# Two attention-fed MLPs on one core: seven early units by way of DRAM for eight, another priority for their loads of x, and one planning dependency of a hidden step

## The chip, the cores and the metric

The kernel runs on one core of a Trainium2 chip. Its time is the device time of one execution in microseconds (us); lower is better. Before the change the median of three runs is 1110.57 us (1105.44 to 1111.51). The engines are TensorE (PE), VectorE (DVE), ScalarE (ACT), GpSimd (POOL) and SyncE (SP, which here only issues DMA).

## The reference: what is computed

A causal attention with a memory term gives x (2304 rows of 512). x goes through a gated MLP of 12 units of 128 hidden columns, and its result through a second MLP of 16 such units.

```python
def reference(**kwargs):                       # cut
    # q, k, v: 4 batches x 8 heads x 576 x 64
    a = softmax(causal(scale * q @ k.T))
    attn_out = g * (phi(q) @ M_prev / (phi(q) @ z_prev)) + (1 - g) * (a @ v)
    x = attn_out.transpose(0, 2, 1, 3).reshape(2304, 512)

    gate = x @ w_gate                          # 512 -> 1536
    x = (gate * sigmoid(gate) * (x @ w_val)) @ w_out

    h = x @ w_in                               # 512 -> 2048
    g = where(h >= 1, h, where(h <= -1, 0, (h + 1) ** 2 / 4))
    return g @ moe2_w_out
```

## The kernel before

**Numbers.** Each fp32 product is made of three float32r matmuls of high and low parts (`PARTS`). The weights come as 64-bit words: a raw tile of 512 KB is loaded (L939), then decoded in some nine small steps, most of them on DVE (L946 to L964, L977, L984; ACT has L944 and L981), into a unit `wu` with a high and a low part.

**Two plans.** The program is written by a list scheduler, `Plan`: operations are added with an engine, an assumed duration, a priority (lower goes first), dependencies and buffer uses. The plan simulates the engines and emits one fixed order per engine; on the chip each engine's queue is in order, and waits are on the data and buffers alone. A dependency given to the plan only for its own sake thus moves an operation in the order and adds no wait on the chip. The first plan holds the attention; of MLP1 it holds the gate and value products of units 0 to 5 for the first three of five token groups (`groups`: 0-512, 512-1024, 1024-1536, 1536-1920, 1920-2304). The second plan holds all that follows, from about 347 us on.

**Early units.** For MLP1's units 0 to `D1`-1, the gate and value products are made early, group by group (`early_unit`): PE multiplies (L1036), ACT copies the result to a tile `gvo` (L1082), and SP stores it to the DRAM tensor `gv[f]` (L1095). In the second plan, the two late groups (1536-1920 and 1920-2304) get units 0 to D1-1, and after them the three groups of 512 get units 6 to D1-1. `load_x` (L1099) loads the four tiles of x (`xb`, 512 KB each for 512 tokens) for a group and tells the plan its priority (L1180). Weight loads of this stretch have priorities from -20 up.

**MLP1** goes in five blocks of tokens (`BLOCKS1`: 512, 512, 384, 384, 512). For each unit, `hidden` makes the hidden tile `h`: a unit below D1 loads its gate and value from `gv` (L1207, `kind` 0, into a buffer of the pool `xb`), a unit from D1 on computes them (L1036, `kind` 1). Then come five steps: ACT (L1230 or L1232), DVE (L1236 or L1238), DVE (L1242 or L1244), ACT's cast (L1248), DVE's low part (L1251). `down` (L1274) multiplies h with w_out and sums in the banks `acc`. At a block's end ACT (L1304) and DVE (L1308) evict, and SP stores y (L1315). The order of units in block 1 is `FIRST`, in the others `fs_last`. The first step of a hidden tile is planned not before the last down but one (L1253).

**MLP2** goes in five blocks (`BLOCKS2`: 512, 512, 512, 384, 384) over 16 units (`kind` 2); its weights are decoded meanwhile, as buffers come free. The result is copied (L1340) and stored (L1343).

Buffers: `xb` 9 (x tiles and gv loads share them), `raw` 3, `hp` (h) 3, `tp` (t) 2, `op` (gvo, yo, oo) 4, four PSUM banks `mm` and four `acc`.

Of the kernel before, what the change touches and what calls it, by code (L numbers as in the profile page):

```python
# [25 lines left out]
NT = B * S  # L26
D0 = 6

D1 = 8
UNITS1 = 12  # L30
EXACT = 4
EXACT_Q = 4
# [49 lines left out]
def f32(ap):  # L82
    return ap.bitcast(F32)
# [160 lines left out]
def c_act(n):  # L244
    return 0.833 * n + 53
# [10 lines left out]
def e_pe(n, cols):  # L256

    return n * (max(cols, 320) + 32) / 2.4
# [6 lines left out]
def e_dve2(n):  # L265
    return 1.04 * n + 157


def e_act(n):
    return 0.833 * n + 194  # L270
# [761 lines left out]
def up_matmuls(nc, out, unit, x, cols, kts=range(KT)):  # L1032

    for kt in kts:
        for i, (pw, px) in enumerate(PARTS):
            nc.tensor.matmul(out, kt_of(unit, pw, kt), x[kt][:, px, cols], start=(kt == 0 and i == 0),  # L1036
                             stop=(kt == KT - 1 and i == 2))
# [3 lines left out]
def tile_attention_two_moe(  # L1041
# [13 lines left out]
    xs = dram.tile([P, KT, 2, NT], F32, name="xs")  # L1055
    ys = dram.tile([P, KT, 2, NT], F32, name="ys")
    gv = [dram.tile([P, 2, NT], F32, name=f"gv{f}") for f in range(D1)]
    tables = {"gate": ({}, moe_w_gate, in_cols), "val": ({}, moe_w_val, in_cols), "wout": ({}, moe_w_out, out_rows)}
# [40 lines left out]
    def load_x(plan, src, pool, tag, tok, prio, deps=()):  # L1099


        n = tok.stop - tok.start
        s = {"x": [None] * KT, "i": [], "t": []}
        last = xlast.get(plan)
        for kt in range(KT):
            i_x = plan.inst(tag)

            def f(kt=kt):
                s["x"][kt] = pool.tile([P, 2, n], F32R, name=tag, tag=tag)
                nc.sync.dma_start(f32(s["x"][kt]), src[:, kt, :, tok])  # L1110

            s["i"].append(i_x)
            s["t"].append(plan.dma(prio, [n * 2.85], f, list(deps[kt]) if deps else [], [i_x], last))
            last = xlast[plan] = plan.last
        return s


    with ExitStack() as actx:
        plan = Plan(over=50)
# [10 lines left out]
        for b in range(B):  # L1130
            t_x[b] = [at.pair(b, n) for n in range(NP)]
            for tok in [g for g in groups if (g.stop - 1) // S == b < B - 1]:
                stored = [[t_x[e][kt] for e in range(tok.start // S, b + 1)] for kt in range(KT)]
                xh = load_x(plan, xs, fpool, "xh", tok, X_AT[b], stored)
# [8 lines left out]
    plan = Plan({"PE": 19000, "ACT": 19000, "DVE": 4000, "POOL": 6000, "DMA": 10000})  # L1143
    UNITS2 = 2 * F2 - UNITS1
    pool = lambda name, bufs: ctx.enter_context(tc.tile_pool(name=name, bufs=bufs, reuse_waits="tile"))
    xb, hp, tp = pool("xb", XB), pool("hp", HP), pool("tp", TP)
# [15 lines left out]

    first = [(kind, f) for f in range(D0, D1) for kind in ("gate", "val")]
    first += [(kind, f) for f in FIRST for kind in ("gate", "val", "wout") if (kind, f) not in ready + first]
# [4 lines left out]
    for i, ((kind, f), tag) in enumerate(zip(first, tags)):  # L1169
        table, w, cut = tables[kind]  # L1170
        table[f] = wts.decode(plan, tag, cut(w, f), -20 if i < 2 * (D1 - D0) else 10 * FIRST.index(f) - 10,
                                act=i >= NOACT)
# [4 lines left out]
        left += [place[x] for x in (("gate", f), ("val", f), ("wout", f)) if x in place]  # L1177
    late = [g for g in groups if (g.stop - 1) // S == B - 1]
    for h, tok in enumerate(late + [g for g in groups if g not in late]):
        xh = load_x(plan, xs, xb, "xb", tok, h - 50 if h < 2 else 22 + h)  # L1180
        for f in [f for f in range(D1) if tok in late or f >= D0]:
            early_unit(plan, mm, f, tok, xh, op, 25 + h, "yo", "op")

# [11 lines left out]
    def hidden(f, tok, base, x, kind, ahead=0):  # L1195


        n = tok.stop - tok.start
        s = {"i": plan.inst("hp")}
        i_t = plan.inst("tp")  # L1200
        src = []
        if kind == 0:
            i_g = plan.inst("xb")

            def load():
                s["gv"] = xb.tile([P, 2, n], F32, name="gv", tag="xb")
                nc.sync.dma_start(s["gv"], gv[f][:, :, tok])  # L1207

            src = [(lambda j=j: s["gv"][:, j], i_g) for j in range(2)]
            t_g = [plan.dma(base - 25, [n * 2.85], load, uses=[i_g], behind=xlast.get(plan))] * 2  # L1210
            xlast[plan] = plan.last
        else:
            units = (gate[f], val[f]) if kind == 1 else (w_in[f],)
            banks = [plan.inst("mm") for _ in units]

            def prod():
                for j, u in enumerate(units):
                    s[j] = mm.tile([P, HT], F32, name="mm", tag=f"mm{banks[j].slot}")
                    up_matmuls(nc, s[j][:, 0:n], u, x["x"], slice(0, n))

            t_g = [plan.add("PE", e_pe(len(units) * 12, n), base + 1 - ahead, prod,
                            [u["t"] for u in units] + x["t"], banks + [u["i"] for u in units] + x["i"],
                            behind=(ups or [None])[-1])]
            ups.append(t_g[0])
            src = [(lambda j=j: s[j][:, 0:n], i_p) for j, i_p in enumerate(banks)]

        def first_step():
            s["t"] = tp.tile([P, n], F32, name="t", tag="t")
            if kind == 2:
                nc.scalar.activation(s["t"], src[0][0](), AF.Relu, bias=half, scale=0.5)  # L1230
            else:
                nc.scalar.activation(s["t"], src[0][0](), AF.Sigmoid)  # L1232

        def second():
            if kind == 2:
                nc.vector.scalar_tensor_tensor(s["t"], s["t"], 1.0, s["t"], op0=ALU.min, op1=ALU.mult)  # L1236
            else:
                nc.vector.tensor_mul(s["t"], src[0][0](), s["t"])  # L1238

        def third():  # L1240
            if kind == 2:
                nc.vector.tensor_max(s["t"], s["t"], src[0][0]())  # L1242
            else:
                nc.vector.tensor_mul(s["t"], s["t"], src[1][0]())  # L1244

        def hi():
            s["h"] = hp.tile([P, 2, n], F32R, name="h", tag="h")
            nc.scalar.copy(s["h"][:, 0], s["t"])  # L1248

        def lo():  # L1250
            nc.vector.tensor_sub(s["h"][:, 1], s["t"], f32(s["h"][:, 0]))  # L1251

        t = plan.add("ACT", e_act(n) + 60, base, first_step, [t_g[0]] + ([] if ahead else downs[-2:-1]), [src[0][1], i_t])  # L1253
        t = plan.add("DVE", e_dve2(n), base, second, [t], [src[0][1], i_t])
        t = plan.add("DVE", e_dve2(n), base, third, [t, t_g[-1]], [src[0][1], src[-1][1], i_t])
        t = plan.add("ACT", e_act(n), base, hi, [t], [i_t, s["i"]])
        s["done"] = plan.add("DVE", e_dve2(n), base, lo, [t], [i_t, s["i"]])
        return s

    ups, downs = [], []  # L1260
# [22 lines left out]
    base = 0  # L1283
    for tok in blocks(BLOCKS1):
        n = tok.stop - tok.start
# [5 lines left out]
        for at_, f in enumerate(fs):  # L1291
            s = hidden(f, tok, base + 10 * at_, x, 0 if f < D1 else 1)

# [4 lines left out]
        for m in range(KT):  # L1298
# [11 lines left out]
            t = plan.add("ACT", c_act(n), base + 110, hi, [t_d], [i_o, i_l, state["i"][m]])  # L1310
# [11 lines left out]
    base = 50000  # L1322
    for tok in blocks(BLOCKS2):
        n = tok.stop - tok.start
# [9 lines left out]
        for m in range(n // P):  # L1334
# [10 lines left out]
            t = plan.add(("ACT", "DVE")[m % 2], c_dve2(DM), base + 200, copy, [t_d], [i_o, state["i"][m]])  # L1345
# [34 lines left out]
```

## Time and profile before

| what | value |
|---|---|
| median of three runs | 1110.57 us (1105.44 to 1111.51) |
| the profiled execution | 1110.57 us |
| its span | 1108.8 us |
| mean granted TensorE clock | 0.995 |
| PE busy | 1076.6 us, 97% of the span |
| DVE, ACT, POOL busy | 756.6, 565.4, 257.0 us |
| DMA, mean over the span | 141 GB/s |

The span is the part of the execution in which the trace has instructions; 1.8 us lie around it. Busy PE is counted from modelled ends of pipelined matmuls, so a row's duration can lap over the next row's start. In the rows of the timeline, what stands in brackets is the idle time of that engine just before the instruction and what ended it. The granted clock is 1.00 at TensorE's upper level of 2.4 GHz and half of that at its lower one.

### The profile page before, as it was taken

The numbers are of one execution on the slowest core, as the hardware profiler recorded it, in microseconds if no ns is written. First come the engines' busy times: TensorE is split into PE (matmuls) and PEld (weight loads), VectorE is DVE, ScalarE is ACT, GpSimd is POOL, SyncE is SP. The second block draws the span as 40 slices with busy tenths as digits, with TensorE's granted clock in tenths as the row PEclk, the third lists the DMA queues.
The fourth block names the chain that finished last, engine by engine and source line by source line (L and its number), as shares of the span: only waits on it lengthen the run. The fifth ranks groups of instructions, "written<-read, shape, count | busy, mean of one in ns | idle before, by whom it ended". The sixth has DMA issues, their size and how long they took to land.

```text
span 1108.8 us, 16480 instructions
## 1 busy us (share of the span) xinstructions
PE 1076.6 (97%) x5520; PEld 924.7 (83%) x5520; DVE 756.6 (68%) x1699; ACT 565.4 (51%) x1286; POOL 257.0 (23%) x325
## 2 busy tenths in 40 slices
PE   6997999999999999999999999999999999999998
PEld 4565788888888998888789997888888888889997
DVE  5688989888983788798945559999433443343433
ACT  6888889999884254544433334454222222222222
POOL 6898669666653000000000000000000000000000
PEclk9999999999999999999999999999999999999999
DMA  5567545765725889976635567361300110110000
GB/s 138 156 172 187 146 123 150 209 165 127 234 91 173 289 302 320 345 235 202 212 104 176 166 221 246 111 236 57 110 1 1 57 39 1 43 39 1 29 1 29
DMA packets 148325, 156.42 MB, mean 141 GB/s; under 512 B 70160, under 2 KB 109072, under 8 KB 148240
## 3 DMA queue, kind: packets, MB, share of 16 engines
q1 hardware_dynamic: 147664, 154.31, 44.8%
q8 instruction: 44, 0.72, 0.3%
q10 hardware_dynamic: 576, 1.05, 0.2%
q14 instruction: 41, 0.34, 0.1%
HBM read 105.78 MB, written 42.47 MB: 134 GB/s over the span
## 4 chain that ended last, share of the span: by engine, by line
PE 50%; DVE 1%; DMA 0%; issue 0%; ACT 0%; DVEq 0%
PE acc L1274 27%; PE mm L1036 23%; DMA ys<-yo 0%; DVE t L1238 0%; DVE h L1251 0%; DVE wA L956 0%; DVE t L1244 0%; DVE wu L984 0%; DVE wA L977 0%; ACT yo L1304 0%; DVE yo L1308 0%; DVE wS L961 0%; DVE wA L949 0%; DVE wA L952 0%; ACT oo L1340 0%
## 5 line engine op out<-in xcount | busy, mean ns | idle before, releaser
L1036 PE MATMUL mm<-xb,wu 128*128 128x512 f32 (+1 forms) x1968 | 410.7, 363 | 0.0
L1036 PEld LDWEIGHTS mm<-xb,wu 128*128 128x128 f32 x1968 | 357.4, 188 | 42.0 <-DVE t L1242 0.2
L1274 PE MATMUL acc<-wu,h 128*128 128x512 f32 x864 | 208.1, 390 | 0.0
L1274 PEld LDWEIGHTS acc<-wu,h 128*128 128x128 f32 x864 | 161.8, 188 | 32.3
L1248 ACT CAST h<-t 128x512 fp32r<-128x512 f32 (+1 forms) x140 | 80.9, 578 | 180.6 <-DVE t L1242 90.1
L1274 PE MATMUL acc<-h,wu 128*128 128x512 f32 (+1 forms) x720 | 152.6, 368 | 2.4 <-DVE h L1251 2.4
L1236 DVE SCALAR_TENSOR_TENSOR t<-t 128x512 f32<-128x512 f32 (+1 forms) x80 | 51.0, 638 | 146.9 <-ACT t L1230 146.9
L1274 PEld LDWEIGHTS acc<-h,wu 128*128 128x128 f32 x720 | 131.0, 188 | 20.5 <-DVE h L1251 3.7
L1251 DVE TENSOR_TENSOR h<-t,h 128x512 fp32r<-128x512 f32 (+1 forms) x140 | 89.0, 636 | 71.8 <-ACT h L1248 71.5
L1230 ACT ACTIVATE t<-mm,half 128x512 f32<-128x512 f32 (+1 forms) x80 | 51.5, 644 | 147.6 <-PE mm L1036 147.2
L1036 PE MATMUL mm<-xh,wu 128*128 128x512 f32 x432 | 115.0, 405 | 1.2 <-DMA xh<-xs 0.9
L755 POOL TENSOR_SCALAR a<-a,r,OGP 128x256 f32<-128x256 f32 (+3 forms) x144 | 96.1, 680 | 28.1 <-DVE r L746 9.7
L1036 PEld LDWEIGHTS mm<-xh,wu 128*128 128x128 f32 x432 | 77.4, 190 | 16.1 <-DMA xh<-xs 1.8
L677 ACT ACTIVATE a<-a,mn 128x128 f32<-128x128 f32 (+3 forms) x128 | 71.0, 558 | 12.7 <-DVE mn L670 12.3
L981 ACT CAST wu<-wA 128x512 fp32r<-128x512 f32 x64 | 39.7, 620 | 52.9 <-DVE wA L977 52.3
L944 ACT ACTIVATE wA<-raw 128x512 f32<-128x512 f32 x64 | 43.2, 675 | 45.3 <-DVE wu L984 20.6
L1082 ACT COPY gvo<-mm 128x512 f32<-128x512 f32 (+1 forms) x80 | 42.9, 544 | 41.3 <-PE mm L1036 40.9
L670 DVE CUSTOM_DVE_ANT_0 a<-s,mask 128x256 f32<-128x256 f32 (+3 forms) x128 | 57.7, 484 | 7.2 <-PE s L664 4.8
L397 DVE TENSOR_TENSOR R<-t,R 128x384 fp32r<-128x384 f32 (+3 forms) x120 | 53.3, 484 | 4.5 <-ACT R L393 3.7
L956 DVE SCALAR_TENSOR_TENSOR wA<-raw,wA 128x512 uint32<-128x512 uint32 x68 | 54.3, 801 | 0.6
L1242 DVE TENSOR_TENSOR t<-t,mm 128x512 f32<-128x512 f32 (+1 forms) x80 | 50.6, 632 | 2.2
L664 PE MATMUL s<-KK,SX 128*128 128x512 f32 (+3 forms) x192 | 42.0, 342 | 8.3 <-DMA KK<-KK 3.5
(134 smaller groups left out, 1401.5 us busy)
## 6 DMA issues: line engine op xcount, KB each, us to landing
raw<-in_moe_w_out_dram SPq DMA_DIRECT2D x28, 512.0 KB, 4.5
xb<-xs SPq DMA_DIRECT2D x24, 512.0 KB, 6.2
gv<-gv SPq DMA_DIRECT2D x24, 512.0 KB, 4.4
gv<-gvo SPq DMA_DIRECT2D x44, 256.0 KB, 4.6
xs<-x SPq DMA_DIRECT2D x16, 576.0 KB, 3.3
raw<-in_moe_w_in_dram SPq DMA_DIRECT2D x16, 512.0 KB
KK<-KK SPq DMA_DIRECT2D x24, 288.0 KB
raw<-in_moe_w_gate_dram SPq DMA_DIRECT2D x12, 512.0 KB, 4.7
```

The lines of the kernel that those rows point to most:

```text
L397: nc.vector.tensor_sub(lo(), src(), f32(hi()))
L670: nc.vector.tensor_tensor_reduce(a, st[f"s{h}{c}"][:, 0:kl], self.mask0[:, 512 - kl:512], -0.125, 3.0e38, ALU.add, ALU.min, mn[:, o:o + 1])
L677: nc.scalar.activation(a, a, AF.Exp, bias=mn[:, o:o + 1], scale=-1.0, accum_out=sm[:, o, 0:1])
L755: nc.gpsimd.tensor_scalar(a, a, st["mn"]["r"][:, o:o + 1], self.OGP[:, n, o:o + 1], op0=ALU.mult, op1=ALU.mult)
L956: nc.vector.scalar_tensor_tensor(s["F"], words(s["raw"])[:, :, 1], 0xC0000000, s["A"], op0=ALU.bitwise_and, op1=ALU.bitwise_or)
L1036: nc.tensor.matmul(out, kt_of(unit, pw, kt), x[kt][:, px, cols], start=(kt == 0 and i == 0), stop=(kt == KT - 1 and i == 2))
L1230: nc.scalar.activation(s["t"], src[0][0](), AF.Relu, bias=half, scale=0.5)
L1236: nc.vector.scalar_tensor_tensor(s["t"], s["t"], 1.0, s["t"], op0=ALU.min, op1=ALU.mult)
L1242: nc.vector.tensor_max(s["t"], s["t"], src[0][0]())
L1248: nc.scalar.copy(s["h"][:, 0], s["t"])
L1251: nc.vector.tensor_sub(s["h"][:, 1], s["t"], f32(s["h"][:, 0]))
L1274: nc.tensor.matmul(state[m][:, 0:o], l, r, start=(f == 0 and i == 0), stop=(f == F - 1 and i == 2), skip_group_check=True)
```

## The change

Three lines are changed. `D1` is 7 instead of 8, so that unit 7's gate and value are no longer made early and stored; each MLP1 block computes them. The loads of x for the second plan's groups have the priority h - 50 for all five groups, where the last three had 22 + h. And a hidden tile's first step is planned not before the last down but two.

```diff
--- before.py
+++ after.py
@@ -26,7 +26,7 @@
 NT = B * S
 D0 = 6
 
-D1 = 8
+D1 = 7
 UNITS1 = 12
 EXACT = 4
 EXACT_Q = 4
@@ -1177,7 +1177,7 @@
         left += [place[x] for x in (("gate", f), ("val", f), ("wout", f)) if x in place]
     late = [g for g in groups if (g.stop - 1) // S == B - 1]
     for h, tok in enumerate(late + [g for g in groups if g not in late]):
-        xh = load_x(plan, xs, xb, "xb", tok, h - 50 if h < 2 else 22 + h)
+        xh = load_x(plan, xs, xb, "xb", tok, h - 50)
         for f in [f for f in range(D1) if tok in late or f >= D0]:
             early_unit(plan, mm, f, tok, xh, op, 25 + h, "yo", "op")
 
@@ -1250,7 +1250,7 @@
         def lo():
             nc.vector.tensor_sub(s["h"][:, 1], s["t"], f32(s["h"][:, 0]))
 
-        t = plan.add("ACT", e_act(n) + 60, base, first_step, [t_g[0]] + ([] if ahead else downs[-2:-1]), [src[0][1], i_t])
+        t = plan.add("ACT", e_act(n) + 60, base, first_step, [t_g[0]] + ([] if ahead else downs[-3:-2]), [src[0][1], i_t])
         t = plan.add("DVE", e_dve2(n), base, second, [t], [src[0][1], i_t])
         t = plan.add("DVE", e_dve2(n), base, third, [t, t_g[-1]], [src[0][1], src[-1][1], i_t])
         t = plan.add("ACT", e_act(n), base, hi, [t], [i_t, s["i"]])
```

How this moves the instructions is shown at five places. First PE at the start of the second plan; `xh` rows are the last products of the first plan, `xb` rows of 384 columns those of the late groups, the first `acc` row the first down of block 1. Before:

```order
L1036 MATMUL mm<-xh,wu 128x512 x54
L1036 MATMUL mm<-xb,wu 128x384 x384
L1036 MATMUL mm<-xb,wu 128x512 x168
L1274 MATMUL acc<-h,wu 128x512 x12
L1036 MATMUL mm<-xb,wu 128x512 x24
L1274 MATMUL acc<-h,wu 128x512 x24
L1036 MATMUL mm<-xb,wu 128x512 x24
```

and with the change:

```order
L1036 MATMUL mm<-xh,wu 128x512 x54
L1036 MATMUL mm<-xb,wu 128x384 x336
L1036 MATMUL mm<-xb,wu 128x512 x120
L1274 MATMUL acc<-h,wu 128x512 x36
L1036 MATMUL mm<-xb,wu 128x512 x24
L1274 MATMUL acc<-h,wu 128x512 x36
L1036 MATMUL mm<-xb,wu 128x512 x24
```

The late groups have 48 matmuls fewer. The row of 512 columns holds, before, two units for each of three groups and one product of block 1 (144 + 24); now it holds one unit for each group and two products of block 1 (72 + 48).

PE at the border of MLP1's first two blocks; the rows `x24` and `x48` of `mm` before the last `acc` row belong to the second block, `acc` rows ahead of them to the first. Before:

```order
L1274 MATMUL acc<-h,wu 128x512 x48
L1036 MATMUL mm<-xb,wu 128x512 x24
L1274 MATMUL acc<-h,wu 128x512 x12
L1036 MATMUL mm<-xb,wu 128x512 x24
L1274 MATMUL acc<-h,wu 128x512 x48
L1036 MATMUL mm<-xb,wu 128x512 x24
```

and with the change:

```order
L1274 MATMUL acc<-h,wu 128x512 x12
L1036 MATMUL mm<-xb,wu 128x512 x24
L1274 MATMUL acc<-h,wu 128x512 x12
L1036 MATMUL mm<-xb,wu 128x512 x48
L1274 MATMUL acc<-h,wu 128x512 x36
L1036 MATMUL mm<-xb,wu 128x512 x24
```

Between the last down of the first block and the first of the second stand 48 products, where 24 stood.

SP, with the numbers of tiles: loads of x (`xb`), of raw weights and stores of early products (`gv<-gvo`) in the groups of 512. Before:

```order
L939 DMA raw_5987<-in_moe_w_out_dram 128x1024
L1095 DMA gv6_75<-gvo_6007 128x512
L939 DMA raw_6024<-in_moe_w_out_dram 128x1024
L1095 DMA gv6_75<-gvo_6022 128x512
L1110 DMA xb_6045<-xs_67 128x2x512
L1110 DMA xb_6048<-xs_67 128x2x512
L1095 DMA gv7_76<-gvo_6061 128x512
L1110 DMA xb_6075<-xs_67 128x2x512
L1110 DMA xb_6078<-xs_67 128x2x512
L1095 DMA gv7_76<-gvo_6073 128x512
L939 DMA raw_6091<-in_moe_w_out_dram 128x1024
```

and with the change, up to block 1's fourth tile (`xb_5986`):

```order
L1110 DMA xb_5899<-xs_67 128x2x512
L1110 DMA xb_5902<-xs_67 128x2x512
L939 DMA raw_5911<-in_moe_w_out_dram 128x1024
L1095 DMA gv6_75<-gvo_5913 128x512
L1110 DMA xb_5930<-xs_67 128x2x512
L1110 DMA xb_5933<-xs_67 128x2x512
L1095 DMA gv6_75<-gvo_5928 128x512
L939 DMA raw_5947<-in_moe_w_out_dram 128x1024
L1110 DMA xb_5958<-xs_67 128x2x512
L1110 DMA xb_5962<-xs_67 128x2x512
L1095 DMA gv6_75<-gvo_5971 128x512
L1110 DMA xb_5986<-xs_67 128x2x512
```

Each group has two stores where it had four, and the loads of x follow each other more closely; xb_5930 and the four after it (xb_5933, xb_5958, xb_5962, xb_5986) are the last tile of the third group and block 1's four.

PE near the end of MLP2's first block, with numbers; `mm_9023` of before and `mm_9002` of now are the product of unit 13, and the `acc` rows are downs. Before, with the first of the downs that follow:

```order
L1036 MATMUL mm_9023<-xb_8316,wu_8826 128x512 x3
L1036 MATMUL mm_9023<-xb_8319,wu_8826 128x512 x3
L1036 MATMUL mm_9045<-xb_8290,wu_8995 128x512 x3
L1036 MATMUL mm_9045<-xb_8311,wu_8995 128x512 x3
L1036 MATMUL mm_9045<-xb_8316,wu_8995 128x512 x3
L1036 MATMUL mm_9045<-xb_8319,wu_8995 128x512 x3
L1274 MATMUL acc_8638<-wu_8599,h_9041 128x512 x3
```

and with the change:

```order
L1036 MATMUL mm_9002<-xb_8151,wu_8996 128x512 x3
L1036 MATMUL mm_9002<-xb_8161,wu_8996 128x512 x3
L1036 MATMUL mm_9002<-xb_8264,wu_8996 128x512 x3
L1036 MATMUL mm_9002<-xb_8272,wu_8996 128x512 x3
L1274 MATMUL acc_8531<-wu_9021,h_9035 128x512 x3
L1274 MATMUL acc_8535<-wu_9021,h_9035 128x512 x3
L1274 MATMUL acc_8539<-wu_9021,h_9035 128x512 x3
L1274 MATMUL acc_8543<-wu_9021,h_9035 128x512 x3
L1036 MATMUL mm_9061<-xb_8151,wu_9055 128x512 x3
```

Before, the product of the next unit and the downs of earlier ones follow on the product of unit 13. Now `h_9035` is unit 13's own hidden tile, made from `mm_9002`; after it comes the product of unit 14 (`mm_9061`), and behind that `h_9093`, unit 14's own, in the same way.

DVE at that place: `t_9118` to `h_9141` are unit 13's hidden tile before, `t_9025` to `h_9035` now; the rest are steps of weights. Before:

```order
L964 SCALAR_TENSOR_TENSOR wS_9098<-raw_8978,wS_9098 128x512
L1236 SCALAR_TENSOR_TENSOR t_9118<-t_9118 128x512
L1251 TENSOR_TENSOR h_9121<-t_9096,h_9121 128x512
L1242 TENSOR_TENSOR t_9118<-t_9118,mm_9023 128x512
L977 TENSOR_TENSOR wA_9058<-wA_9058,wS_9098 128x512
L1251 TENSOR_TENSOR h_9141<-t_9118,h_9141 128x512
```

and with the change:

```order
L956 SCALAR_TENSOR_TENSOR wA_9015<-raw_8913,wA_9015 128x512
L1236 SCALAR_TENSOR_TENSOR t_9025<-t_9025 128x512
L961 TENSOR_SCALAR wS_9031<-wA_9015 128x512
L1242 TENSOR_TENSOR t_9025<-t_9025,mm_9002 128x512
L964 SCALAR_TENSOR_TENSOR wS_9031<-raw_8913,wS_9031 128x512
L949 TENSOR_SCALAR wA_9028<-wA_9028 128x512
L1251 TENSOR_TENSOR h_9035<-t_9025,h_9035 128x512
```

The chain's three steps stood with one step of a neighbour's chain and one of a decode between them; now three steps of decodes stand between them.

## Rows read from the trace of the kernel before

**Rows 1.** first part of the page: busy us (share) xinstructions

```profile
PE 1076.6 (97%) x5520; PEld 924.7 (83%) x5520; DVE 756.6 (68%) x1699; ACT 565.4 (51%) x1286; POOL 257.0 (23%) x325
```

**Rows 2.** windows of core 0: stretch, its length, then by column

```profile
core 0: us, PE busy (x) PEld busy (x) DVE busy (x) ACT busy (x) POOL busy (x), PEclk, DMA share, GB/s
...
0.00:347.00 347.00, 321.57 (x1911) 264.79 (x1912) 285.65 (x850) 300.19 (x820) 255.55 (x324) 0.99 0.57 156
...
347.00:1104.00 757.00, 754.58 (x3610) 659.88 (x3610) 470.47 (x850) 264.62 (x465) 1.44 (x1) 1.00 0.40 134
...
425.00:450.00 25.00, 25.00 (x115) 20.95 (x113) 19.76 (x38) 11.92 (x21) 0.00 (x0) 1.00 1.03 376
...
440.00:464.00 24.00, 24.00 (x107) 19.89 (x106) 17.83 (x34) 11.98 (x20) 0.00 (x0) 1.00 1.02 384
```

**Rows 3.** waits, 347 to 1109 us: who, us in total, times, longest

```profile
PE acc L1274 <- DVE h L1251: 2.4, 2, 1.4
```

**Rows 4.** timeline of PE: start, us, instruction, [idle before]

```profile
360.02 104.87 PE L1036 MATMUL mm<-xb,wu 128*128 128x384 f32 x552
...
464.73 2.88 PE L1274 MATMUL acc<-h,wu 128*128 128x512 f32 x12
...
536.95 5.74 PE L1274 MATMUL acc<-h,wu 128*128 128x512 f32 x24 [0.98 <-DVE h L1251]
```

**Rows 5.** chain that ended last, in order of time: start, us, what

```profile
590.84 4.16 PE mm L1036 x24
...
761.23 5.44 PE mm L1036 x24
```

**Rows 6.** timeline of all engines, one hidden chain of MLP2

```profile
815.46 2.88 PE L1036 MATMUL mm<-xb,wu 128*128 128x512 f32 x12
...
818.18 2.88 PE L1274 MATMUL acc<-wu,h 128*128 128x512 f32 x12
...
818.44 0.69 ACT L1230 ACTIVATE t<-mm,half 128x512 f32<-128x512 f32 x1 [2.65 <-PE mm L1036]
...
819.16 0.69 DVE L1236 SCALAR_TENSOR_TENSOR t<-t 128x512 f32<-128x512 f32 x1 [2.65 <-ACT t L1230]
...
821.27 0.69 DVE L1251 TENSOR_TENSOR h<-t,h 128x512 fp32r<-128x512 f32 x1 [0.69 <-ACT h L1248]
```

**Rows 7.** timeline of DVE near the first hidden tile

```profile
462.84 0.42 DVE L949 TENSOR_SCALAR wA<-wA 128x512 f32<-128x512 f32 x1
...
463.18 0.68 DVE L1251 TENSOR_TENSOR h<-t,h 128x512 fp32r<-128x512 f32 x1
```

**Rows 8.** timeline of PE in the attention, and the windows behind

```profile
94.52 0.75 PE L863 MATMUL av<-PP,MZ 128*64 128x320 f32 x2 [2.05 <-ACT PP L505]
...
110.89 1.30 PE L664 MATMUL s<-KK,SX 128*128 128x256 f32 x4 [2.85 <-DVE mn L670]
...
94.00:97.00 3.00, 2.48 (x10) 1.40 (x11) 2.50 (x6) 2.93 (x9) 2.31 (x4) 1.00 0.92 228
...
110.00:116.00 6.00, 4.82 (x24) 4.30 (x25) 5.89 (x18) 4.58 (x15) 1.28 (x1) 0.72 0.29 87
```

**Rows 9.** timeline of SP's queue: x loads

```profile
424.20 0.88 SPq L1110 DMA_DIRECT2D xb<-xs  x2
```

**Rows 10.** DMA issues: xcount, KB each, median us to landing

```profile
xb<-xs SPq DMA_DIRECT2D x11, 512.0 KB, 6.2
...
gv<-gv SPq DMA_DIRECT2D x24, 512.0 KB, 4.4
```

**Rows 11.** DVE's decodes: the first step, and all ends up to 458

```profile
366.63 0.43 DVE L946 TENSOR_SCALAR wA<-raw 128x512 uint32<-128x512 uint32 x1 [18.10 <-DMA raw<-in_moe_w_gate_dram]
...
L984 DVE TENSOR_TENSOR wu<-wA,wu x21: 682/685/694, 372.6 to 457.4; 128x512 fp32r<-128x512 f32 x21
```

## Prediction

> **What bounds the kernel now.** I read the page first: TensorE is busy for 97% of the span [rows 1]. The windows say where the other 3% lies: up to 347 us, in the attention part, PE is busy 321.57 of 347 us, and from 347 to 1104 us 754.58 of 757 [rows 2]. The change touches nothing before the second plan, so all it can win lies in the second window, and the list of PE's waits there has one entry that counts: two waits of the down products for a hidden tile, 2.4 us together [rows 3]. The timeline places the first, 0.98 us at 536.95, at the start of MLP1's second block [rows 4]; the second, 1.4 us, stands at the start of the last one. The number of PE's matmuls stays at 5520. **The kernel is a full queue of matmuls, and the change can gain at most about 2.4 us; it can lose wherever it sets a matmul right behind something that isn't ready.** So I went through PE's order for places where a product is followed at once by the down that needs it, and through the front of the second plan for inputs that come later than PE.
>
> **What the change removes.** Ten ACT copies, ten stores of gv and five loads of gv go. None ends a PE wait in [rows 3], and the 120 matmuls go to other places at the same pace (24 of 512 columns take 5.44 us, 24 of 384 columns 4.16 us, [rows 5]), so by itself this is 0.
>
> **Block starts: -2.4.** After the last down of an MLP1 block, PE now has 48 matmuls of up products before the first down of the next, where it had 24: at 5.44 us for 24 [rows 5] the hidden chain gets 10.9 us for 5.4. The waits of before were 0.98 and 1.4 us, so 5.4 more covers both. Bounds 0 and -2.4; I take -2.4, since what ended both was this chain.
>
> **Two bare pairs in MLP2's first block: +8.4.** This is the largest term. Near the end of that block the order now has the product of unit 13, then at once its own down, then the product of unit 14 and at once its own down. PE's queue is in order, so each time PE stands still from the end of the product to the end of the hidden chain. The chain has five steps (ACT, DVE, DVE, ACT, DVE). A bare copy of it with PE's end is in the timeline of the last blocks: the product of twelve ends where the next PE group starts, at 818.18, ACT's step starts at 818.44, DVE's at 819.16, and DVE's last one, at 821.27, ends 0.69 later at 821.96 [rows 6]: 3.8 us. In MLP2's first block DVE also decodes weights, and by its order three small decode steps stand between the steps of the chain of unit 13. Two such steps start 0.34 us apart where a short one leads [rows 7]; one before the second DVE step counts in full, the others partly fill the 0.7 us in which DVE waits for ACT's cast. I take 4.2 for each pair, 8.4 together. Lower bound 2 x 3.8 = 7.6; upper, with two more steps of a decode ahead, 2 x 4.8 = 9.6. No other work hides this: before, the down of unit 13 came behind five other groups. Nor do I see a place later where PE's loss is given back, since PE has no other wait.
>
> **The clock: +3.4.** An idle PE can lose clock. After an idle of 2.85 us (row 110.89) the granted clock over the six us from 110 is 0.72, which is 0.28 x 6 = 1.7 us lost, the lower level being 1.2 of 2.4 GHz; after one of 2.05 us (row 94.52) it stays at 1.00 [rows 8]. The two waits of 4.2 are longer than the first of these, so I take 2 x 1.7. But before 110.89 PE had been busy with gaps, and here with none, so 0 is the other end. The Trainium skill, TensorE: Matmul & The Clock Gate, Part 1, says that the half rate is the state at rest and that activity lifts it. [...]
>
> **The front: +4.5.** Seven blocks by way of DRAM instead of eight leave each of the three groups of 512 tokens one early unit (24 matmuls, 5.44 us) instead of two. PE's dates after the change follow from [rows 4, 5]: the second plan's first matmul at 360.02, 14 units of 384 columns at 4.16 to 418.3, three groups of 5.44 to 434.6, then the products of block 1's units 8 and 9 to 445.4, where the first down stands (464.73 before). PE wants the fourth tile of block 1's x nine matmuls after 434.6, at 434.6 + 9 x 0.227 = 436.6.
>
> The x loads have the new priority, but xb has nine buffers: only one load really passes weight loads, the others wait until PE frees a tile. The first that waits for the end of the late groups was issued at 424.20 [rows 9], where those groups ended at 360.02 + 16 x 4.16 = 426.6, so 2.4 us ahead; now that is 415.9. From there to block 1's fourth tile SP's order has eleven loads of x (5.77 MB), three raw weight loads (1.57 MB), two stores of 192 KB (0.39 MB) and three of 256 KB (0.79 MB): 8.52 MB. In the two windows where DMA has no gap it moves 376 and 384 GB/s [rows 2]; at 380 this takes 22.4 us, and with about 3.0 us that a load takes beyond its transfer (4.4 us of landing for 512 KB of gv [rows 10] less 1.4 of transfer) the tile lands at 441.3, 4.7 us late. I take 4.5, in several waits. The lower bound is 0: the load could be issued at 429.3, when PE frees its buffer, and the median landing of an x load is 6.2 us [rows 10], which is 435.5. The upper bound is 6, if the stores of unit 6 hold SP's queue. By the Trainium skill, DMA: Bandwidth & Descriptors, section Where 436 GB/s comes from, the fabric's ceiling is 435 GB/s: 19.6 us and a wait of about 2; the same section's limit of some 358 GB/s for HBM makes 23.8 us and 6. The windows lie above the second and below the first.
>
> **DVE in the front: 0 beside the wait for x.** 17 units are to be decoded ahead of the first hidden tile (21 before). DVE starts on them at 366.63; 21 ends of decodes lie from 372.6 to 457.4 [rows 11], 4.24 us apiece. The 17th ends at 372.6 + 16 x 4.24 + 0.7 = 441.1, and the first hidden tile, which was done at 463.18 + 0.68 [rows 7], 5.8 us behind the 21st, at 446.9: 1.5 us after 445.4. With the wait for x PE comes later than that, so it costs nothing; without it, 1.5. That raw loads start one x load (1.4 us) later is hidden in the same way.
>
> **Sum.** -2.4 + 8.4 + 3.4 + 4.5 = +13.9. The profiled execution took 1110.57 us (span 1108.8 and 1.8 around it) and is itself the median of the runs shown, so the forecast is **1124.5 us**.
>
> **Rivals.**
> B, the clock holds: PE has no gap for hundreds of us ahead of the pairs, and the idle of 2.05 us was forgiven. Against it, 4.2 is beyond the idle that wasn't. 1124.5 - 3.4 = 1121.1.
> C, the loads of x are in time: what the Trainium skill's 435 GB/s in the section named above would bring near. For it, the lower bound by landing times; against it, both windows. Then DVE's 1.5 us shows in place of 4.5: 1121.5.
> E, decodes fall behind: MLP2's evictions of block 4 come some 11 us earlier in the order, and behind them stand fewer decoded units (by DVE's order 34 of 56 where 37 were). If two units are late when PE wants them, 2 x 4.3 = 8.6 more: 1133. For it, DVE is the second busiest engine [rows 2]; against it, the waits show no PE wait for a decode today [rows 3].
> D, the other side, not slower: the traffic that goes frees the front. Unit 7's stores of five groups (2.36 MB) are 6.2 us of transfers at 380 GB/s. If that lets block 1's fourth tile land by 436.6 with the decodes moved up too, and the short idles leave the clock as at 94.52, only the bare pairs stay: -2.4 + 7.6 = +5.2, 1115.8. It decides at 0.35 us: with more than that left over it is slower.
> F, the title holds and the pairs are covered, because the chain of unit 13 starts on the product's first half or PE's order does not bind: -2.4, 1108.2. Against it, PE issues in order, and the chain reads a whole tile.
>
> **How the numbers follow.** Forecast A 0.45 (1124.5), B 0.17 (1121.1), C 0.15 (1121.5), E 0.10 (1133), D 0.09 (1115.8), F 0.04 (1108.2). The range leaves out E, F and little else: its low end is D's 1115.5, its high end A with both upper bounds, 1124.5 + 1.2 + 1.5 + 2.8 for a clock that falls in the front too, 1130. Half a per cent is 5.55 us, about what a measurement of this kernel can tell from no change. D and F lie within it, so same has 0.13; A, B, C and E are slower by more, 0.86; faster than by 0.5% (under 1105.0) would need more than PE's whole idle time in the second window, 0.01.
>
> **What would show it.** PE's waits of the profile after: no wait at the starts of MLP1's second and last block; two of about 4.2 us for DVE's last hidden step, one after the other and some 3 us apart, in MLP2's first block; granted clock under 0.9 in the six us behind them; waits for DMA of xb of 4 to 5 us between 418 and 445 us, and the first down near 450. If the pairs' waits are absent or under 3 us each, the main term is wrong; if PE waits for a weight's decode in MLP2, E is right.

## The result

The changed kernel takes 1123.44 us (median of six runs, 1120.75 to 1125.75), that of before 1110.29 us beside it: a ratio of 1.0129, with a 95% interval from 1.0109 to 1.0149. It is slower by 13.2 us; the forecast was 1124.5 us, 13.9 more than before. The profiled execution took 1125.75 us, with a span of 1124.0; it is the slowest of the six. One of the twelve executions of the last experiment's kernel took 2748.91 us at a granted clock of 1.00, where the others took 1099.52 to 1107.83; it is left out of that kernel's numbers, and its cause is open.

The first part of the page of the changed kernel, to be held against [rows 1]:

```profile
PE 1085.8 (97%) x5520; PEld 930.8 (83%) x5520; DVE 756.4 (67%) x1699; ACT 562.7 (50%) x1276; POOL 257.1 (23%) x325
```

PE's count of matmuls is the same. Two groups of the second plan now carry idle time: products that waited for a load of x, and downs of MLP2 that waited for DVE's last hidden step. So says the list of waits from 347 us on (total, times, longest), where [rows 3] had one entry:

```profile
PE acc L1274 <- DVE h L1251: 7.9, 2, 4.0
...
PE mm L1036 <- DMA xb<-xs: 2.7, 3, 1.5
```

The two waits of before at MLP1's block starts are gone. To see what each stretch lost I leave out the attention part, whose code is the same, and count from the second plan's first matmul (the first row of 384 columns): before it takes 1108.8 - 360.02 = 748.8 us to the end of the span, now 1124.0 - 360.40 = 763.6. **The 14.8 us are the front, +6.8, the two bare pairs with their clock, about +10.9, and the block starts, about -2.8** (rounded; these make 14.9); the runs below part them.

**The front.** PE's timeline there (start, us, instruction, idle before):

```profile
360.40 75.89 PE L1036 MATMUL mm<-xb,wu 128*128 128x384 f32 x411
437.81 0.97 PE L1036 MATMUL mm<-xb,wu 128*128 128x512 f32 x3 [1.53 <-DMA xb<-xs]
439.11 1.11 PE L1036 MATMUL mm<-xb,wu 128*128 128x512 f32 x3 [0.33 <-DMA xb<-xs]
441.10 11.72 PE L1036 MATMUL mm<-xb,wu 128*128 128x512 f32 x39 [0.88 <-DMA xb<-xs]
452.65 8.32 PE L1274 MATMUL acc<-h,wu 128*128 128x512 f32 x36
```

From 360.40 to the first down at 452.65 are 92.25 us. The matmuls in it would take 336 x 0.1733 + 120 x 0.2267 = 85.4 at the pace of [rows 5], so 6.8 are lost: 2.74 in the three waits for x, and most of the rest to the clock, as the 39 matmuls behind the last wait show, which took 11.72 us instead of about 9.

**The pairs.** PE's timeline near the end of MLP2's first block:

```profile
783.73 2.88 PE L1036 MATMUL mm<-xb,wu 128*128 128x512 f32 x12
790.59 4.61 PE L1274 MATMUL acc<-wu,h 128*128 128x512 f32 x12 [3.97 <-DVE h L1251]
795.03 2.91 PE L1036 MATMUL mm<-xb,wu 128*128 128x512 f32 x12
801.92 4.45 PE L1274 MATMUL acc<-wu,h 128*128 128x512 f32 x12 [3.97 <-DVE h L1251]
```

Each product of twelve is followed by its own down after 3.97 us of standing. The hidden chain of the first pair, on ACT and DVE, from the timeline of all engines:

```profile
786.65 0.69 ACT L1230 ACTIVATE t<-mm,half 128x512 f32<-128x512 f32 x1 [1.78 <-PE mm L1036]
...
787.37 0.69 DVE L1236 SCALAR_TENSOR_TENSOR t<-t 128x512 f32<-128x512 f32 x1 [1.16 <-ACT t L1230]
787.98 0.42 DVE L961 TENSOR_SCALAR wS<-wA 128x512 uint32<-128x512 uint32 x1
788.31 0.68 DVE L1242 TENSOR_TENSOR t<-t,mm 128x512 f32<-128x512 f32 x1
...
789.03 0.62 ACT L1248 CAST h<-t 128x512 fp32r<-128x512 f32 x1 [1.13 <-DVE t L1242]
789.51 0.42 DVE L949 TENSOR_SCALAR wA<-wA 128x512 f32<-128x512 f32 x1
...
789.85 0.68 DVE L1251 TENSOR_TENSOR h<-t,h 128x512 fp32r<-128x512 f32 x1
```

It is the chain of [rows 6] with decode steps between its own: L961 stands ahead of the second DVE step and costs 0.3 us in full; L949, and an L964 not shown, fill the time of ACT's cast and cost little. The windows behind these waits and behind the front's (columns as in [rows 2]):

```profile
440.00:446.00 6.00, 5.12 (x13) 3.89 (x13) 3.87 (x8) 4.18 (x6) 0.00 (x0) 0.50 1.05 400
...
791.00:797.00 6.00, 6.00 (x21) 4.74 (x20) 5.36 (x11) 1.93 (x3) 0.00 (x0) 0.72 0.20 74
802.00:806.00 4.00, 4.00 (x12) 3.18 (x13) 3.82 (x7) 0.67 (x2) 0.00 (x0) 0.63 0.02 4
```

The granted clock is 0.50, the lower level, from 440 to 446 us, which takes in the end of the last wait for x, and 0.72 and 0.63 in the windows behind the pairs.

### The profile page after: what moved, and what is told of

It is laid out like the page before. It is cut to its first block, busy times and chain, and to the rows that moved or that the text cites. A ratio compares the mean times of both kernels' runs of the same rounds, so it can differ in the third digit from the quotient of the medians.

```text
span 1124.0 us, 16421 instructions
## 1 busy us (share of the span) xinstructions
PE 1085.8 (97%) x5520; PEld 930.8 (83%) x5520; DVE 756.4 (67%) x1699; ACT 562.7 (50%) x1276; POOL 257.1 (23%) x325
## 4 chain that ended last, share of the span: by engine, by line
PE 85%; DMA 6%; ACT 5%; DVE 2%; issue 1%; SPq 1%; ACTq 0%; DVEq 0%
PE mm L1036 40%; PE acc L1274 31%; PE av L863 6%; PE s L664 2%; DMA KK<-KK 1%; PE t L802 1%; PE s L660 1%; ACT a L677 1%; DMA raw<-in_moe_w_gate_dram 1%; DMA xh<-xs 1%; DMA xb<-xs 1%; DMA gv<-gvo 1%; PE s L698 1%; ACT R L393 1%; ACT KK L393 1%
## 5 line engine op out<-in xcount | busy, mean ns | idle before, releaser
L1274 PE MATMUL acc<-wu,h 128*128 128x512 f32 x864 | 211.5, 395 | 7.9 <-DVE h L1251 7.9
L1082 ACT COPY gvo<-mm 128x512 f32<-128x512 f32 (+1 forms) x70 | 37.5, 544 | 43.9 <-PE mm L1036 41.4
L956 DVE SCALAR_TENSOR_TENSOR wA<-raw,wA 128x512 uint32<-128x512 uint32 x68 | 51.8, 761 | 0.5
```

What stands on the lines that cost most here:

```text
L956: nc.vector.scalar_tensor_tensor(s["F"], words(s["raw"])[:, :, 1], 0xC0000000, s["A"], op0=ALU.bitwise_and, op1=ALU.bitwise_or)
L1274: nc.tensor.matmul(state[m][:, 0:o], l, r, start=(f == 0 and i == 0), stop=(f == F - 1 and i == 2), skip_group_check=True)
```

## The experiments

The first number of each is device time, with the ratio to runs of before on the same chip beside it; the medians of before beside these runs lie between 1107.5 and 1109.0 us. Since the attention part differs from execution to execution (last section), the profiles are compared from the second plan's start. That stretch is 748.8 us for before and 763.6 for the changed kernel. The edits are shown shortened. Seven and eight "blocks" in these texts are the early units kept in DRAM (`D1`), not blocks of tokens.

### The step edit put back

```diff
-downs[-3:-2]          # in the changed kernel
+downs[-2:-1]
```

> The changed kernel with only the planning dependency of the hidden step put back as before (seven blocks and the loads' priority stay). PE's order then has no down right behind its own product in MLP2's first block, and the front is as in the changed kernel. If the bare pairs and the clock behind them cost what the trace after shows (two waits of 3.97 us and about 3.2 us of clock): 1123.4 - 11.1 = 1112.3 us, with the waits for x and the low clock at 440 us still there and no wait at the starts of MLP1's blocks. Rival, the loss comes with the seven blocks themselves (evictions and decodes that move up) and the pairs only show it: another wait takes their place in MLP2's first block, 1119 us or more.

Measured: 1111.60 us, 1.0037 of before (1.0022 to 1.0052). PE's only waits from 347 us on, and PE's rows at the ends of the front:

```profile
PE mm L1036 <- DMA xb<-xs: 2.4, 3, 1.6
```

```profile
358.98 75.81 PE L1036 MATMUL mm<-xb,wu 128*128 128x384 f32 x411
...
451.00 5.60 PE L1274 MATMUL acc<-h,wu 128*128 128x512 f32 x24
```

No other wait took the place of the pairs, and the front lost nearly the same (92.02 us to the first down, with the clock at 0.50 from 438 to 444 us). From the first down to the end are 660.5 us, where the changed kernel has 671.35: the pairs and the clock behind them cost 10.9 us. From the second plan's start it is 752.5, so seven early units without the pairs lose 3.7 us: the front's 6.6 less 2.8 that the block starts gave back.

### The step edit alone

```diff
-([] if ahead else downs[-2:-1])     # in the kernel before
+([] if ahead else downs[-3:-2])
```

> The kernel before with only the planning dependency of the hidden step changed (eight blocks, loads as before). In MLP2's first block PE's order has one group of twelve matmuls (2.72 us) between the product of unit 14 and its own down, and no bare pair. By the theory that a pair costs the hidden chain less its cover: one wait of 3.97 - 2.72 = 1.25 us, no fall of the clock behind it, the wait at MLP1's second block (0.98) gone, that of the last block (1.39) still there as its cover is unchanged: 1110.3 + 1.25 - 0.98 = 1110.6 us. Rival, the step edit by itself makes the loss, however large the cover: 1118 us or more.

Measured: 1110.13 us, 1.0023 (1.0007 to 1.0040). From the second plan's start it is 750.8 us, 2.0 more than before where 0.3 was expected, and the parts are others. Both block starts were free of waits, also that of the last block; unit 14's down didn't wait, because the product between, that of unit 15, itself did:

```profile
785.25 0.51 PE L1036 MATMUL mm<-xb,wu 128*128 128x512 f32 x1 [2.75 <-ACT wu L981]
786.14 3.99 PE L1036 MATMUL mm<-xb,wu 128*128 128x512 f32 x11 [0.38 <-DVE wu L984]
```

```profile
786.00:790.00 4.00, 3.86 (x12) 3.09 (x13) 3.53 (x7) 0.00 (x0) 0.00 (x0) 0.68 0.46 135
```

What PE waited for is the cast of unit 15's weights and the last step of their decode. This is the rival of late decodes (E), at a third of its price, with a fall of the clock (0.68) behind 3.1 us of idle. So the step edit alone is no source of 13 us, but in MLP2 it takes PE to a place where DVE isn't yet. Nor do the parts add up: 2.0 us here and 3.7 for seven early units with the old step make 5.7, and together they cost 14.8, since the two bare pairs stand in PE's order only when both are there.

### Fewer bytes in the front

```diff
+nc.gpsimd.memset(f32(s["x"][kt])[:, :, P:n], 0.0)            # block 1's x alone
-nc.sync.dma_start(f32(s["x"][kt]), src[:, kt, :, tok])
+nc.sync.dma_start(f32(s["x"][kt])[:, :, 0:P], src[:, kt, :, part])
```

> The changed kernel, but the four loads of x for MLP1's first block bring 128 of 512 columns each (393 KB less apiece; GpSimd, idle there, sets the other columns to zero, so that block's units 7 to 11 are computed from partly empty tiles). PE's order is the changed kernel's. If the waits in the front are a matter of bytes, 1.57 MB less is 4.1 us at 380 GB/s and covers the 2.7 us of waits; if the low clock from 440 to 446 us comes from these waits, it goes too: 1123.4 - 2.7 - 3.5 = 1117.2 us; with DVE's decodes showing as the next limit, up to 1.5 us more, 1118.7. Rival, the waits are set by when buffers come free and SP's queue, and the bytes matter little: 1122 to 1123.4, waits for x as before.

Measured: 1121.24 us, 1.0121 (1.0089 to 1.0153). The waits for x shrank to one of 0.23 us and the clock there stayed at 1.00; the first down stood 86.1 us behind the second plan's start. But the next thing was late at once (the lines of code stand five further down here, L1279 is the down):

```profile
445.17 3.01 PE L1279 MATMUL acc<-h,wu 128*128 128x512 f32 x12
450.05 5.74 PE L1279 MATMUL acc<-h,wu 128*128 128x512 f32 x24 [1.86 <-DVE h L1256]
```

The second and third down waited 1.86 us for DVE; the first hidden tile, for which I had worked out 1.5 us, was in time. SP issued block 1's fourth tile of x at the same date behind the second plan's start in both kernels, 71.6 us (the changed one, first row) and 71.7 (here):

```profile
431.98 0.36 SPq L1110 DMA_DIRECT2D xb<-xs  x1
```

```profile
430.76 0.36 SPq L1113 DMA_DIRECT2D xb<-xs  x1
```

So what buffers and SP's queue decide did not move, and the waits went all the same: the bytes were the cause of the waits for x, and DVE is the limit just behind them. The pairs were as before, 3.98 us each. The total fell by 3.3 us in the profile (760.35 for 763.6) and not by the 4.7 to 6.2 expected, since that wait came up and the clock fell further behind the first pair (the down took 5.24 us for 4.61). That fall differs between executions of one kernel too (5.39 in the changed kernel's second profile, whose stretch is 762.1 us), so the gain is 1.8 to 3.3 us, and the device times, whose intervals overlap, don't show it.

### More bytes in the front

```diff
 nc.sync.dma_start(gv[f][:, j, tok], s["o", j])
+if f == 6: nc.sync.dma_start(gx[:, j, tok], s["o", j])   # second plan, step edit put back
```

> The changed kernel with the step's planning dependency as before (no bare pairs), and every store of unit 6's early products in the second plan issued twice, the second time to a DRAM tensor that nobody reads. PE's order is that of the run without the step edit. Between the first load that waits for the late groups and block 1's fourth tile of x this puts two stores of 192 KB and three of 256 KB more, 1.18 MB or 3.1 us at 380 GB/s. If the wait for x is a matter of bytes: 2.4 us of waits in the run without doubled stores become about 5.5, the first down stands 3 us later behind the second plan's start (92.0 there, 95 here), with the clock low behind the waits again. Rival, the buffers and SP's queue set the dates: waits as there, first down at 92 to 93 us.

Measured, one execution: 1116.37 us.

```profile
PE mm L1036 <- DMA xb<-xs: 6.2, 5, 2.1
```

```profile
357.28 67.31 PE L1036 MATMUL mm<-xb,wu 128*128 128x384 f32 x375
...
453.32 5.60 PE L1280 MATMUL acc<-h,wu 128*128 128x512 f32 x24
```

The waits for x grew from 2.4 to 6.2 us, and the first down stands 96.0 us behind the start for 92.0. Both are 4 us or a little less, where 3.1 was worked out. The clock is low again (0.74 from 443 to 449 us). By itself this run doesn't part the bytes from SP's queue, since the fourth tile was also issued later (77.8 us behind the start for 71.5); the run of fewer bytes does. Together they show the mechanism: the loads of x are late by the bytes that are to be moved up to them.

### One pair covered

```diff
-([] if ahead else downs[-3:-2])     # in the changed kernel
+([] if ahead else (downs[-3:-2] if kind < 2 else downs[-2:-1]))
```

> The changed kernel with the step edit in MLP1 alone. PE's order differs from the changed kernel's in MLP2's first block only: one down of an earlier unit (twelve matmuls, 2.72 us) now stands between unit 13's product and its own down, while unit 14's down still stands right behind its product. If a pair costs the hidden chain less its cover, and the clock falls only behind the long wait: unit 13's wait 3.97 - 2.72 = 1.25 us, with the granted clock at 1.00 behind it; unit 14's 3.97, with the clock low behind it; from the first down to the end 2.7 + 1.6 = 4.3 us less than the 671.4 us of the changed kernel. Rival, the time goes wherever the decodes are late and the order doesn't matter: 671 us as there.

Measured, one execution: 1115.86 us (its attention part was the shortest seen, so the total says little). From the first down to the end are 667.85 us for 671.35.

```profile
781.74 3.01 PE L1274 MATMUL acc<-wu,h 128*128 128x512 f32 x12 [1.53 <-DVE h L1251]
...
792.05 4.44 PE L1274 MATMUL acc<-wu,h 128*128 128x512 f32 x12 [4.58 <-DVE h L1251]
```

```profile
782.00:788.00 6.00, 5.47 (x24) 4.16 (x23) 5.15 (x11) 1.81 (x3) 0.00 (x0) 1.00 0.28 87
792.00:796.00 4.00, 3.95 (x11) 3.17 (x12) 3.90 (x7) 0.62 (x1) 0.00 (x0) 0.60 0.02 4
```

With 2.72 us of another down in between, unit 13's wait is 1.53 us instead of 3.97, and the clock behind it stays at 1.00. Unit 14's pair, unchanged in PE's order but with other steps between its own on DVE and ACT, waits 4.58, with the clock at 0.60 behind it. A pair costs the chain less its cover; the gain is 3.5 us of the 4.3 expected, since the second wait was 0.6 longer.

### The loads' priority alone

```diff
-h - 50 if h < 2 else 22 + h         # in the kernel before
+h - 50
```

> The kernel before with only the priority of the x loads changed. PE's order is that of before, word for word; on SP and DVE some loads and decode steps trade places. By the theory this part does nothing: 1.000 of before within the interval, waits of 0.98 and 1.39 us at the block starts as before. Rival, the loads that go ahead delay raw weights and with them the first hidden tile: a wait of PE near 460 us and 2 us or more slower.

Measured: 1107.64 us, 0.9995 (0.9983 to 1.0008). PE's waits are those of before (2.4 us, two of them), and the second plan takes 748.5 us. By itself this part of the change does nothing that can be measured; with seven early units it was not taken apart.

### The changed kernel again

> The changed kernel once more, on the chip and beside the runs of before of this call. The theory says that its profile repeats itself in all that lies behind the attention part: two pair waits of 3.97 us, x waits of 2.4 to 2.8 us near 437 us with the clock low behind them, about 763.6 us from the second plan's start to the end of the span, 1.013 of before. Rival, that the clock behind the pairs was an accident of one execution: 760 us or less.

Measured: 1123.12 us, 1.0139 (1.0116 to 1.0163). From the second plan's start 762.1 us. The pairs repeat: 3.98 us each, the clock low behind both. The front's waits repeat too (3.2 us in all), but not its clock; PE's row behind the last wait for x and the window there:

```profile
437.33 9.14 PE L1036 MATMUL mm<-xb,wu 128*128 128x512 f32 x39 [1.01 <-DMA xb<-xs]
```

```profile
438.00:444.00 6.00, 6.00 (x28) 4.96 (x27) 4.59 (x9) 4.26 (x6) 0.00 (x0) 1.00 1.05 393
```

The 39 matmuls take 9.14 us where they took 11.72. The first down comes 89.9 us behind the start instead of 92.25. So of the front's 6.8 us some 2.4 hang on the clock of the execution. The low clock is the commoner case: the front is the same in the runs with the step edit put back and with one pair covered, and at like waits (2.4 and 2.6 us) the clock there is 0.50 too (438 to 444 us and 434 to 440 us).

### A longer cover in MLP1, twice

```diff
-([] if ahead else downs[-2:-1])     # in the kernel before
+([] if ahead else (downs[-4:-3] if kind < 2 else downs[-2:-1]))
```

> The kernel before (eight blocks, loads as before) with the planning dependency of the hidden step moved to the last down but three, and in MLP1 alone; MLP2's stays as before. PE's order then has 48 products or more at the starts of MLP1's second and last block, where it had 24, and the least cover of a hidden chain anywhere is as before. If that is all that the step edit is good for: both waits (0.98 and 1.39 us) go and nothing else moves, 1110.3 - 2.4 = 1107.9 us. Rival, the moved steps collide with decodes on DVE and another wait of 2 us or more comes up: 1110 us or above.

Measured: 1102.84 us, 0.9955 (0.9937 to 0.9973).

> The kernel before with the planning dependency of the hidden step at the last down but three in MLP1 alone, once more, with more runs. From the second plan's start to the end its profile took 745.3 us where that of before took 748.8, so the theory (the two waits at block starts, each with some 0.3 us for draining and filling PE, and nothing else) gives 1110.3 - 3.0 to 3.5, a ratio of 0.997; the attention part ahead of it is the same code and what its executions differ by is no effect. Rival, the first result (0.9955) holds a gain in the attention part that the second plan's code gives: again 0.9955 or less, with the second plan starting at 356 us or sooner where before starts at 360.

Measured: 1104.56 us, 0.9970 (0.9955 to 0.9984). PE has no wait at all in the second plan in either profile; in the second one, whose span is 1102.7 us, its rows at the ends of the front are:

```profile
357.46 104.87 PE L1036 MATMUL mm<-xb,wu 128*128 128x384 f32 x552
462.18 2.88 PE L1274 MATMUL acc<-h,wu 128*128 128x512 f32 x12
```

From the second plan's start they take 745.3 and 745.2 us for 748.8. This version is faster than both kernels: 3.5 us, or 0.3%, less than before by the second run and by its profile. The first one's 4.7 us is no contradiction, as the two intervals overlap. That it is 3.5 us and not the 2.4 of the two waits is in part that PE loses more at a wait than its idle row. PE's rows around the two waits of before:

```profile
530.37 5.60 PE L1274 MATMUL acc<-h,wu 128*128 128x512 f32 x24
...
669.58 5.60 PE L1274 MATMUL acc<-h,wu 128*128 128x512 f32 x24
676.57 5.75 PE L1274 MATMUL acc<-h,wu 128*128 128x512 f32 x24 [1.39 <-DVE h L1251]
```

The downs behind the second wait start 6.99 us after those ahead of them, where a group of 24 takes 5.44, and take 5.75 us themselves for 5.60. That is 1.7 us for an idle row of 1.39, and in the same way 1.3 for the other, at 536.95; 0.5 us stay unexplained.

### The change's own step edit in MLP1 alone, with eight early units

```diff
-([] if ahead else downs[-2:-1])     # in the kernel before
+([] if ahead else (downs[-3:-2] if kind < 2 else downs[-2:-1]))
```

> The kernel before with the planning dependency at the last down but two (as in the change) in MLP1 alone; MLP2's stays as before. PE's order has 48 products at the start of MLP1's second block, 24 as before at that of the last. Theory: the wait of 0.98 goes, that of 1.39 stays, no wait for a decode in MLP2: 1.3 us less than before (0.98 and some 0.3 for draining and filling), a ratio of 0.999. Rival, what the step edit alone showed in MLP2 (2.75 us for a unit's cast and a low clock behind it) comes from PE being early there and not from the order of MLP2's own steps: the same wait here, 1 us slower than before or more.

Measured: 1104.54 us (median of eleven), 0.9967 (0.9951 to 0.9984), 745.5 us from the second plan's start. Both expectations missed: the wait in MLP2 didn't come, and the wait at the last block's start went too, although only 24 products stand there. So its cause was not the cover alone. Before, DVE's and ACT's timelines ahead of that wait:

```profile
669.08 0.62 ACT L1232 ACTIVATE t<-gv 128x512 f32<-128x512 f32 x1
```

```profile
668.85 0.78 DVE L949 TENSOR_SCALAR wA<-wA 128x512 f32<-128x512 f32 x2
669.55 0.76 DVE L952 TENSOR_SCALAR wA<-wA 128x512 uint32<-128x512 uint32 x2
670.22 1.29 DVE L956 SCALAR_TENSOR_TENSOR wA<-raw,wA 128x512 uint32<-128x512 uint32 x2
671.42 0.42 DVE L961 TENSOR_SCALAR wS<-wA 128x512 uint32<-128x512 uint32 x1
671.88 0.69 DVE L964 SCALAR_TENSOR_TENSOR wS<-raw,wS 128x512 f32<-128x512 uint32 x1
672.49 0.68 DVE L1238 TENSOR_TENSOR t<-gv,t 128x512 f32<-128x512 f32 x1
...
675.83 0.68 DVE L1251 TENSOR_TENSOR h<-t,h 128x512 fp32r<-128x512 f32 x1
```

ACT had done the first step of the hidden tile by 669.70. DVE, whose order is fixed, did eight decode steps from 668.85 on before it came to the second step at 672.49, 2.8 us later, and the last step ended at 676.51, just before PE went on (676.57). The wait was a hidden step that stood behind decodes. With the edit the same tile's second and last steps on DVE stand at the border ahead of those decodes, and PE's three downs run through:

```profile
658.69 0.69 DVE L1238 TENSOR_TENSOR t<-gv,t 128x512 f32<-128x512 f32 x1
...
661.17 0.69 DVE L1251 TENSOR_TENSOR h<-t,h 128x512 fp32r<-128x512 f32 x1
```

```profile
658.48 5.64 PE L1036 MATMUL mm<-xb,wu 128*128 128x512 f32 x24
663.97 8.32 PE L1274 MATMUL acc<-h,wu 128*128 128x512 f32 x36
```

The tile is ready at 661.86, before the downs begin. The edit starts the tile's whole chain sooner, ACT's step too, so that its place in DVE's queue was what counted is read from the queue of before; no run moved that place alone.

## Why the prediction was right

**Bare pairs, +8.4: right in place, cause and size.** Two waits of 3.97 us, 7.9 together, for DVE's last hidden step, with decode steps between the chain's own as the order had them. With the step edit put back 10.9 us go, the clock behind them included.

**Clock behind the pairs, +3.4: right.** The downs behind them took 4.61 and 4.45 us for 2.88, 3.3 us together. In the second profile they took 5.39 and 4.52, 4.2 together. The Trainium skill, TensorE: Matmul & The Clock Gate, Part 1, has activity lift the clock from a state of rest. That it fell behind these idle times fits. Single idle rows of 1.39, 1.53 and 1.86 us cost no clock here.

**The front, +4.5: the mechanism right, the parts mis-sized.** The fourth tile of block 1's x was met at 441.10 (441.3 was forecast), where PE wanted it at 437.0. But only 2.74 us of that were idle rows, in three waits, as PE was held up at the tiles before too and lost some 1.4 us more around them; and then the clock was low, which the sum had at 0 and the range had as an upper bound. The front lost 6.8 us in one profile of the changed kernel, 4.4 in the other. DMA moved 390 GB/s from 418 to 442 us in the changed kernel and 407 from 425 to 445 with the doubled stores. The Trainium skill, DMA: Bandwidth & Descriptors, Where 436 GB/s comes from, gives two limits, some 358 GB/s for HBM and 435 for the fabric. Both rates lie between them.

**DVE behind x, 1.5: near in size, at another tile.** Once x was in time, PE waited 1.86 us for DVE, but ahead of the second and third down; the first hidden tile, which the prediction had 1.5 us late, was not.

**Block starts, -2.4: right in size (-2.8), wrong in cause.** The step that failed is "the hidden chain gets 10.9 us for 5.4". With more cover the waits are gone (the run with the step edit put back). But both waits of before stood ahead of the new block's third and fourth down, with two downs (5.44 us, the rows at 530.37 and 669.58) between them and the 24 products, so that the chain had more than 5.4 us already. At the last start it was late since it stood behind decodes on DVE, and the step edit in MLP1 removes both waits with eight early units as before and no more than 24 products there. I had read the waits at PE and counted cover, and not followed the chain to DVE's queue.

**The rivals.** D and F fell with the pairs and the front. B, the clock holds, fell at the pairs in every profile; in the front the clock held in one of four. C fell: bytes did matter. E was not in the changed kernel, and came up at a third of its price in the step edit alone.

The sum's +13.9 against +14.8 in the profile and +13.2 between medians: the pairs and their clock came out 1 us below (even in the second profile), the front 2.3 above (even in the second), the block starts 0.4 below. That the sum is closer than its terms is luck: in the first profile their errors cancel, and the cause of one of them was wrong.

## What to carry to other kernels

Where the bounding engine is full, read a change of plan for the places where an instruction comes to stand right behind what it needs: the whole chain is then paid in full, and the clock on top, and such a place can be found in the instruction order before anything runs. Take a wait back to the queue in which its chain stands, not only to the engine that waits; a step that is ready and stands behind work with time to spare needs a new place, not more cover. And try the parts of a change apart, and together: here one part, the loads' priority, did nothing by itself, seven early units with it lost 3.7 us and the step edit 2.0, both lost 14.8 together, and the step edit kept out of MLP2 gained 3.3.

## What was not expected of the hardware

**The same waits don't always cost clock.** The front of the changed kernel had 2.7 us of waits with the clock at 0.50 from 440 to 446 us in one profile, and 3.2 us with the clock at 1.00 in the other; two other kernels with this front lost the clock as the first did. What decides it is open. The pairs, with waits of 3.97 us, lost clock in every profile.

**The attention part is not constant.** Its order is the same in all these kernels, and the second plan started between 354.5 and 360.4 us in twelve profiles, an interval larger than most effects here. Over the whole span the granted clock was 0.995 where it started at 360.0 and 0.998 where it started at 355.2, but 0.995 also where it started at 357.5; the cause is open.
